# Linear attention feeding a gated MLP on one core: 128-row products for plain q and rest tokens, x normalised by pair, dependent transfers moved back in their queue

## The chip, the cores and the metric

The kernel runs on one core of one Trainium2 chip. A core has five engines, each with its own queue of instructions worked off in order: TensorE (PE, matrix products; PEld is its loading of weights), VectorE (DVE), ScalarE (ACT), GpSimd (POOL) and SyncE (SP), which here issues all DMAs. The metric is the device time of one execution in microseconds (us), as the median of several runs. The profile is of one further execution.

## The reference

Linear attention over 8 batches x 8 heads of 576 tokens with 64 features each, and then a gated MLP without an activation:

```python
def phi(x):
    proj = np.einsum('bhsd,df->bhsf', x, w_phi)                 # 64 -> 128 features
    proj = proj - np.max(np.abs(proj), axis=-1, keepdims=True)
    return np.concatenate([np.exp(proj), np.exp(-proj)], axis=-1)
q_p, k_p = (phi(q), phi(k))
kv = np.einsum('bhsf,bhsd->bhfd', k_p, v)
num = np.einsum('bhsf,bhfd->bhsd', q_p, kv)
den = np.einsum('bhsf,bhf->bhs', q_p, np.sum(k_p, axis=2))[..., None] + 1e-06
x = (num / den)                       # heads side by side: 4608 tokens x 512
out = (x @ w_a) * (x @ w_b) @ w_out   # 512 -> 1536 -> 512
```

All of it is in float32. The last three arrive as 64-bit numbers, which the kernel decodes to float32 itself.

## The kernel before

**Precision.** A product is either plain (float32 operands, each product two records on TensorE) or split: an operand is cut into a high and a low part (`split`, L146, with ScalarE's cast at L142 and VectorE's subtraction at L149; `stack`, L151, cuts one whose two copies lie in the two halves of the rows), and three products stand for one. The first 9 of 32 pairs of heads have plain k, q and numerators (`PLAIN_K`, `PLAIN_Q`, `PLAIN_NUM`, L38), the first 11 a plain kv.

**Attention.** It goes by pairs of heads (`attention_steps`, L386). For a pair, `k_chunks` (L258) makes features of k for 512 tokens in two chunks of 256 and adds their products with v to one PSUM tile `kvps` (`kv_add`, L292). The remaining 64 tokens of two pairs, the rest tokens, are put together as 128 rows (`rest_load`, `rest_chunk`): rows 0 to 63 are the first pair's, 64 to 127 the second's. `rest_add` (L280) takes one half of the rows, so these products have 64 rows. `k_finish` (L305) copies `kvps` (kvT), transposes it (`pt`, L314) and copies it again (kvh, L317). `q_side` (L325) goes by head: it loads q (L333; one transfer of 64 rows where q is plain, two copies in two transfers where it is split), multiplies with `w_phi` (`pq`, L346, 64 rows where plain), takes the greatest absolute value on GpSimd (`mb`, L350), subtracts it (L351), makes both exponentials (L354), multiplies with kv (`pn`, L370) and writes the numerators to `xun` and the denominators to `den`, both in DRAM. `reciprocals` (L376) loads a pair's denominators, inverts them and writes `rec` to DRAM.

**First pass of the MLP.** `load_weights` decodes the first 6 of 12 slices of w_a, w_b and w_out (18 tensors). `moe_block` (L566) works on 288 tokens, 16 blocks in all: `load_x` (L553) loads four chunks of x (`x_chunk`, L534: x unnormalised from `xun`, and `rec` broadcast over 64 rows in two transfers, then one multiplication on VectorE, L550) and splits them; for each slice `pa` and `pb` take 24 products (L583), are multiplied (L588) and split into hh and hl; then four output tiles `po` (L609) are summed, copied to `o` by ScalarE (L617), and the four are written to `part` in DRAM with one transfer (L624).

**Second pass.** The other 6 slices, on 512 tokens at a time, with Winograd's seven products (`second_pass`, L705; `winograd`, L660; x again through `x_chunk`, in `factors_of_x`, L626). Its weights are decoded and combined by `load_factors` while the last five blocks of the first pass run, partly set down in DRAM (`keep`) and fetched back (`fetch`). Its first tile `top` (L680) takes memory that the first pass's buffers held.

**What sets the order.** Attention is planned by hand in turns: a pair every 5 turns at first, then every 4; the constants at L24 to L35 give the turn of each step. Steps of the MLP are put into a deque and taken out at `PACE0` and then `PACE` steps a turn. Decoding is put there at turn 2, the two blocks of a batch `BLOCK_LAG` turns after its last pair's last step. This is the order in which the program names its instructions. The framework then sorts every engine's queue by a simulated timeline, an instruction named earlier going first among those that are ready, and the hardware works the queues off in that order.

Of the kernel before, what the change touches and what calls it, by code (L numbers as in the profile page):

```python
# [19 lines left out]
P = 128  # L20
EPS = 1e-6
# [12 lines left out]
DECODE_TURN, X_LAG, BLOCK_LAG = 2, 2, 8  # L34
PACE0, PACE, PACE0_UNTIL = 0.65, 0.9, 18  # L35
# [24 lines left out]
def tile_kernel(ctx, tc, qT, km, kr, vm, vr, w_phi, w_a, w_b, w_out, out):  # L60
# [14 lines left out]
    B, H, _, S = qT.shape  # L75
# [19 lines left out]
    rec = [dpool.tile([H, S], F32, name=f"rec{b}") for b in range(B)]  # L95
    part = dpool.tile([DM, NT], F32, name="part")
# [14 lines left out]
    def attention_consts(a1):  # L111
# [17 lines left out]
        make_identity(nc, ident)  # L129
        vaug = []  # L130
# [4 lines left out]
        return w2, wh, wl, wk32, wk2, ident, vaug  # L135
# [20 lines left out]
    def k_load(b, pr, a1, a2, ps, consts, st):  # L156
# [4 lines left out]
        if i < PLAIN_K:  # L161
            k32 = a1.tile([P, n], F32, tag="ks", bufs=2, name=f"k32_{u}")
            nc.sync.dma_start(k32, km[b, pr])
# [25 lines left out]
    def rest_load(b, g, a1, a2, ps, consts, st):  # L189
# [21 lines left out]
        if i >= PLAIN_KV:  # L211
            vh = a1.tile([P, 2, D + 1], F32R, tag="rvh", name=f"rvh_{u}")
            vl = a1.tile([P, 2, D + 1], F32R, tag="rvl", name=f"rvl_{u}")
            split(vh, vl, v32, engine("v_hi", b), engine("v_lo", b))
            st["rv", b, g] = (vh, vl)
# [109 lines left out]
    def q_side(b, pr, j, a1, a2, ps, consts, st):  # L325
        w2, wh, wl = consts[:3]
# [4 lines left out]
        q32 = a2.tile([P, S], F32, tag="q32", name=f"q32_{u}")  # L331
        for i in range(1 if plain_q else 2):
            nc.sync.dma_start(q32[i * D : (i + 1) * D], qT[b, h])  # L333
        yield
        if plain_q:
            parts = [(w2[:D], q32[:D])]
# [14 lines left out]
        engine("q_sub", b).tensor_tensor(p32, p32, mb, op=ALU.subtract)  # L351
# [20 lines left out]
        nc.sync.dma_start(xun[b][h * D : (h + 1) * D], xn[:D])  # L372
        nc.sync.dma_start(den[b][h : h + 1], xn[D : D + 1])
        yield

    def reciprocals(b, pr, a1):  # L376
        n = 2 * S // P
        hs = slice(2 * pr, 2 * pr + 2)
        r = a1.tile([P, n], F32, tag="rec", bufs=2, name=f"r_{b}_{pr}")
        nc.sync.dma_start(r, den[b][hs].rearrange("h (a n) -> (h a) n", n=n))  # L380
        nc.vector.tensor_scalar_add(r, r, EPS)
        nc.vector.reciprocal(r, r)
        nc.sync.dma_start(rec[b][hs].rearrange("h (a n) -> (h a) n", n=n), r)
        yield

    def attention_steps(pools, consts, st):  # L386
# [7 lines left out]
        for i in range(B * NPAIR):  # L394
# [13 lines left out]
            plan(reciprocals(b, pr, pools[0]), [t0 + Q_STEP + Q_TURNS[-1]])  # L408
            if b == 0:
                plan(x_first, [t0 + Q_STEP + Q_TURNS[-1] + X_LAG])  # L410
            if pr == NPAIR - 1:
                plan(b, [t0 + Q_STEP + Q_TURNS[-1]])
# [93 lines left out]
    def stage_shared(pool):  # L506

        def stage(kind, shape, dt, name):
            if kind == "raw":
                return xpool.tile(shape, dt, tag="o", bufs=2, name=name)  # L510
# [4 lines left out]
    def stage_second(xin, pool):  # L515

        tags = {"raw": (pool, "raw"), "w": (xin, "xs"), "w32": (xin, "rb"), "ws": (xin, "xs")}
# [16 lines left out]
    def x_chunk(p, j, c, pool, bufs):  # L534
# [3 lines left out]
        rb = pool.tile([P, T], F32, tag="rb", bufs=2, name=f"rb_{u}_{c}")  # L538

        t = j * T  # L540
        while t < (j + 1) * T:
            b, s0 = divmod(t, S)
            n = min(S - s0, (j + 1) * T - t)
            src, dst = slice(s0, s0 + n), slice(t - j * T, t - j * T + n)
            nc.sync.dma_start(x32[:, dst], xun[b][c * P : (c + 1) * P, src])
            for i in range(2):
                h = 2 * c + i
                nc.sync.dma_start(rb[i * D : (i + 1) * D, dst], rec[b][h : h + 1, src].broadcast_to([D, n]))
# [322 lines left out]
```

## Time and profile before

| | us |
|---|---|
| median of 3 runs | 1280.15 |
| lowest, highest | 1278.54, 1281.26 |
| profiled execution: span from first to last instruction | 1276.4 |
| TensorE busy | 1237.6 |
| TensorE loading weights | 1136.8 |
| VectorE busy | 928.9 |
| ScalarE busy | 733.0 |
| GpSimd busy | 155.4 |

The profiled execution is given by its span alone; the time of a run has a few microseconds more around it. Busy time of TensorE counts a record from its start to its modelled end, and records overlap: how close products follow each other is read from the times at which they start. A row such as `pq<-q,w 64*128 64x288` is a product into `pq` with weights of 64 rows and 128 columns, over 288 columns of data. A wait is written `<-` with the engine, the tile and the line that ended it.

### The profile page before, as it was taken

What the parts mean: (1) busy time and instruction counts of PE and PEld (TensorE: products, weight loads), DVE (VectorE), ACT (ScalarE), POOL (GpSimd) and SP (SyncE); (2) the same over time, 40 slices, a digit from 0 to 9 for tenths busy, and PEclk for the clock granted to TensorE, in tenths of its full rate; (3) what the DMA queues carried; (4) which work ended last, traced back from release to release, by engine and by line L of the source; (5) the groups of instructions that cost most, each with busy time, mean ns of one, the idle gap of its engine ahead of it and who ended that gap; (6) DMA issues with size and microseconds to landing.
All of it is one profiled execution on the core that took longest, in us unless ns stands there. A gap on an engine that the chain in (4) does not pass through costs nothing.

```text
span 1276.4 us, 23144 instructions
## 1 busy us (share of the span) xinstructions
PE 1237.6 (97%) x8588; PEld 1136.8 (89%) x8588; DVE 928.9 (73%) x1682; ACT 733.0 (57%) x1577; POOL 155.4 (12%) x70
## 2 busy tenths in 40 slices
PE   7899999999999999999999999889999999999998
PEld 4566789899999999999999999789999999999997
DVE  6989567998889999988965886824656556456443
ACT  5667668888888888988874444413223223223221
POOL 2332121212222221312220000000000000000000
PEclk9999999999999999999999999999999999999999
DMA  8665443353434434444225576791422322331221
GB/s 186 173 182 154 120 129 92 99 151 82 140 98 131 120 93 134 108 116 121 70 57 165 151 241 230 236 299 48 127 84 72 116 91 66 109 100 50 66 67 50
DMA packets 136656, 157.13 MB, mean 123 GB/s; under 512 B 40864, under 2 KB 93600, under 8 KB 136544
## 3 DMA queue, kind: packets, MB, share of 16 engines
q1 hardware_dynamic: 136544, 155.66, 42.4%
q8 instruction: 67, 1.10, 0.3%
q14 instruction: 45, 0.37, 0.1%
HBM read 117.56 MB, written 38.04 MB: 122 GB/s over the span
## 4 chain that ended last, share of the span: by engine, by line
PE 62%; DVE 14%; DMA 13%; ACT 6%; issue 4%; SPq 1%; DVEq 0%; ACTq 0%
PE pab L674 21%; PE po L721 11%; PE pa L583 6%; PE pb L583 5%; PE kvps L292 5%; PE po L609 5%; PE pn L370 4%; DMA x<-xun 3%; DMA rb<-rec 2%; PE pq L346 2%; DVE kd L240 1%; DMA raw_b<-in_w_b 1%; DVE qs L154 1%; DMA r<-den 1%; DVE kel L149 1%
## 5 line engine op out<-in xcount | busy, mean ns | idle before, releaser
L350 POOL PARTITION_ALL_REDUCE mb<-p x64 | 154.7, 2418 | 497.4 <-ACT p L347 463.2
L583 PE MATMUL pb<-xh,wh_b 128*128 128x288 f32 x384 | 115.6, 301 | 5.9 <-ACT o L617 2.9
L583 PE MATMUL pa<-xh,wh_a 128*128 128x288 f32 x384 | 116.0, 302 | 0.7 <-ACT xh L142 0.4
L583 PE MATMUL pb<-xh,wl_b 128*128 128x288 f32 x384 | 115.0, 299 | 0.0
L583 PE MATMUL pa<-xh,wl_a 128*128 128x288 f32 x384 | 115.0, 299 | 0.0
L609 PE MATMUL po<-hh,wh_o 128*128 128x288 f32 x384 | 110.3, 299 | 4.3 <-ACT hh L142 2.4
L583 PE MATMUL pa<-xl,wh_a 128*128 128x288 f32 x384 | 113.7, 296 | 0.0
L583 PE MATMUL pb<-xl,wh_b 128*128 128x288 f32 x384 | 113.3, 295 | 0.0
L609 PE MATMUL po<-hl,wh_o 128*128 128x288 f32 x384 | 112.2, 296 | 1.1 <-DVE hl L149 1.0
L609 PE MATMUL po<-hh,wl_o 128*128 128x288 f32 x384 | 112.4, 297 | 0.0
L142 ACT CAST hh<-h 128x288 fp32r<-128x288 f32 (+1 forms) x150 | 72.6, 503 | 68.7 <-DVE h L588 40.5
L149 DVE TENSOR_TENSOR hl<-h,hh 128x288 fp32r<-128x288 f32 (+1 forms) x150 | 81.7, 557 | 19.8 <-ACT hh L142 19.5
L550 DVE TENSOR_TENSOR x<-x,rb 128x288 f32<-128x288 f32 (+1 forms) x100 | 56.3, 567 | 53.4 <-DMA x<-xun 38.3
L583 PEld LDWEIGHTS pb<-xh,wh_b 128*128 128x128 f32 x384 | 72.6, 189 | 8.4 <-ACT h L587 4.6
L583 PEld LDWEIGHTS pa<-xh,wh_a 128*128 128x128 f32 x384 | 72.5, 189 | 4.6 <-issue 1.9
L609 PEld LDWEIGHTS po<-hh,wh_o 128*128 128x128 f32 x384 | 70.7, 188 | 5.9 <-ACT hh L142 3.1
L609 PEld LDWEIGHTS po<-hl,wh_o 128*128 128x128 f32 x384 | 72.4, 189 | 2.5 <-DVE hl L149 1.7
L583 PEld LDWEIGHTS pa<-xl,wh_a 128*128 128x128 f32 x384 | 73.4, 191 | 0.6 <-issue 0.2
L583 PEld LDWEIGHTS pa<-xh,wl_a 128*128 128x128 f32 x384 | 72.7, 189 | 1.3 <-issue 1.1
L583 PEld LDWEIGHTS pb<-xl,wh_b 128*128 128x128 f32 x384 | 73.4, 191 | 0.3
L583 PEld LDWEIGHTS pb<-xh,wl_b 128*128 128x128 f32 x384 | 72.8, 189 | 0.6 <-issue 0.6
L609 PEld LDWEIGHTS po<-hh,wl_o 128*128 128x128 f32 x384 | 71.9, 188 | 0.8 <-issue 0.8
(272 smaller groups left out, 3833.3 us busy)
## 6 DMA issues: line engine op xcount, KB each, us to landing
q<-in_qT SPq DMA_DIRECT2D x110, 144.0 KB
k<-in_km SPq DMA_DIRECT2D x55, 256.0 KB
xun<-xn SPq DMA_DIRECT2D x64, 144.0 KB
x<-xun SPq DMA_DIRECT2D x64, 144.0 KB
rb<-rec SPq DMA_DIRECT2D x128, 72.0 KB
part<-o SPq DMA_DIRECT2D x16, 576.0 KB
o<-part SPq DMA_DIRECT2D x36, 256.0 KB
out_x<-o SPq DMA_DIRECT2D x36, 256.0 KB
```

Source lines behind the costliest of these rows:

```text
L142: eng.copy(dst, src)
L149: eng_lo.tensor_tensor(lo, src, hi, op=ALU.subtract)
L154: eng_lo.tensor_tensor(hi_lo[D:], src[D:], hi_lo[D:], op=ALU.subtract)
L292: nc.tensor.matmul(st["kv_ps", b, pr][:width, j], v_[:, j, :width], e_[:, j], start=(left == NFULL and j == 0 and n_ == 0), stop=(left == ...
L346: nc.tensor.matmul(pq[:, :HALF], w_, q_[:, tok], start=(n_ == 0), stop=(n_ == len(parts) - 1))
L350: nc.gpsimd.partition_all_reduce(mb, p32, P, bass_isa.ReduceOp.absmax)
L370: nc.tensor.matmul(pn[: D + 1, :HALF], kv_[:, 2 * j + s, :], e_[:, s, tok], **at)
L550: nc.vector.tensor_tensor(x32, x32, rb, op=ALU.mult)
L583: nc.tensor.matmul(acc, w[:, cc * P : (cc + 1) * P], x, start=(k == 0), stop=(k == 3 * NCC - 1))
L609: nc.tensor.matmul(accs[cc], w[:, cc * P : (cc + 1) * P], h, **at)
L674: nc.tensor.matmul(acc[to][:, i], w_, x_, skip_group_check=True, **at)
L721: nc.tensor.matmul(acc[cc], w[:, cc * P : (cc + 1) * P], h, **at)
```

## The change

- Plain q: the two heads of a pair are loaded as one tile of 128 rows (`qP`), and multiplied with `wz[:, j]`, a copy of w_phi that is zero in the other head's rows (the tile that plain k already uses). Split q: the two copies come from the host as one tensor (`qD`) and one transfer.
- Rest tokens: v comes from the host with zeros in the other pair's 64 rows (`vr` has one more axis of 2), into two tiles that stay (`rvz`), and `rest_add` takes all 128 rows.
- x: `reciprocals` becomes seven steps. It loads the denominators, inverts them, writes `rec`, loads the pair's numerators (128 rows of 576), loads `rec` broadcast to the same shape, multiplies, and writes `xnorm` to DRAM. `x_chunk` loads from `xnorm` alone, in both passes. For this `xun` holds the two heads' rows in turn, and the host turns the rows of w_a and w_b the same way.
- Each of these transfers is named with `behind(loads, ...)`, and the two VectorE steps with `behind(marks, ...)`: `tc.issue_after` puts them behind the latest load of q or k, or the latest subtraction of q, in the queue of the same engine. It is an order in the queue and no wait on a semaphore. Steps lie up to 8 turns behind the pair's last step (2 in the first and the last batch).
- First pass: a block loads the next block's x while its own third slice runs (three chunks, the fourth when the first is split) and splits it among its outputs; `o` holds two output tiles and is written twice a block. The first block takes the decoding of w_out among its own steps; raw weights go through other buffers (qe and qel). Blocks are put in the deque 9 turns after a batch's last step (3 in the first and the last batch; before 8), at a `PACE` of 1.0 instead of 0.9.

```diff
-DECODE_TURN, X_LAG, BLOCK_LAG = 2, 2, 8
-PACE0, PACE, PACE0_UNTIL = 0.65, 0.9, 18
+REC_TURNS0, REC_TURNS, X_TURNS = (0, 1, 1, 1, 2, 2), (1, 3, 4, 5, 7, 8), (0, 1)
+DECODE_TURN, BLOCK_LAG = 2, 1
+PACE0, PACE, PACE0_UNTIL = 0.65, 1.0, 18
...
+        rvz = []
+        for i in range(2):
+            t = a1.tile([P, 2, 2, D + 1], F32, name=f"rvz{i}")
+            nc.vector.memset(t, 0.0)
+            for r in range(2):
+                nc.vector.memset(t[r * REST : (r + 1) * REST, r, :, D : D + 1], 1.0)
+            rvz.append(t)
...
-        v32 = a1.tile([P, 2, D + 1], F32, tag="rv32", name=f"rv32_{u}")
-        nc.vector.memset(v32[:, :, D : D + 1], 1.0)
-        nc.sync.dma_start(v32[:, :, :D], vr[b, g])
+        v32 = consts[6][g % 2]
+        nc.sync.dma_start(v32[:, :, :, :D], vr[b, g])
...
-        rows = slice(pr % 2 * REST, (pr % 2 + 1) * REST)
-        kv_add(b, pr, [v_[rows] for v_ in st["rv", b, pr // 2]], [e_[rows] for e_ in st["re", b, pr // 2]], st)
+        kv_add(b, pr, [v_[:, pr % 2] for v_ in st["rv", b, pr // 2]], st["re", b, pr // 2], st)
...
-            parts = [(w2[:D], q32[:D])]
+            parts = [(wz[:, j], st["q", b, pr])]
...
-        engine("q_sub", b).tensor_tensor(p32, p32, mb, op=ALU.subtract)
+        marks.append(nc.vector.tensor_tensor(p32, p32, mb, op=ALU.subtract))
...
+    def behind(what, issue):
+        with tc.issue_after(what[-1].ins):
+            issue()
...
         r = a1.tile([P, n], F32, tag="rec", bufs=2, name=f"r_{b}_{pr}")
-        nc.sync.dma_start(r, den[b][hs].rearrange("h (a n) -> (h a) n", n=n))
-        nc.vector.tensor_scalar_add(r, r, EPS)
+        behind(loads, lambda: nc.sync.dma_start(r, den[b][hs].rearrange("h (a n) -> (h a) n", n=n)))
+        yield
+        behind(marks, lambda: nc.vector.tensor_scalar_add(r, r, EPS))
         nc.vector.reciprocal(r, r)
-        nc.sync.dma_start(rec[b][hs].rearrange("h (a n) -> (h a) n", n=n), r)
+        yield
+        behind(loads, lambda: nc.sync.dma_start(rec[b][hs].rearrange("h (a n) -> (h a) n", n=n), r))
+        x32 = a1.tile([P, S], F32, tag="x32", name=f"x32_{b}_{pr}")
+        nc.sync.dma_start(x32, xun[b][rows])
+        yield
+        rb = a1.tile([P, S], F32, tag="rb", name=f"rb_{b}_{pr}")
+        behind(loads, lambda: nc.sync.dma_start(rb, rec[b][hs].unsqueeze(0).broadcast_to([D, 2, S])))
+        yield
+        behind(marks, lambda: nc.vector.tensor_tensor(x32, x32, rb, op=ALU.mult))
+        yield
+        behind(loads, lambda: nc.sync.dma_start(xnorm[b][rows], x32))
         yield
...
-            nc.sync.dma_start(x32[:, dst], xun[b][c * P : (c + 1) * P, src])
-            for i in range(2):
-                h = 2 * c + i
-                nc.sync.dma_start(rb[i * D : (i + 1) * D, dst], rec[b][h : h + 1, src].broadcast_to([D, n]))
+            nc.sync.dma_start(x32[:, t - j * T : t - j * T + n], xnorm[b][c * P : (c + 1) * P, s0 : s0 + n])
             t += n
-        nc.vector.tensor_tensor(x32, x32, rb, op=ALU.mult)
...
+            if f == 2 and j + 1 < blocks[0]:
+                loaded = [x_chunk(p, j + 1, c, pool, 3) for c in range(3)]
...
         for cc in range(NCC):
+            if loaded:
+                x_make(p, j + 1, cc, loaded.pop(0), pool)
+                if cc + 3 < NCC:
+                    loaded.append(x_chunk(p, j + 1, cc + 3, pool, 3))
             outputs(cc, range(NFS[p] - 1 if cc < ahead else 0, NFS[p]))
...
+            if cc % 2 == 0:
+                o = pool.tile([P, 2, T], F32, tag="o", bufs=2, name=f"o_{p}_{j}_{cc}")
+            nc.scalar.copy(o[:, cc % 2], acc)
+            if cc % 2:
+                nc.sync.dma_start(dst[:, cc - 1 : cc + 1], o)
...
+    def first_block(block, decodes):
+        for steps in decodes:
+            yield from steps
+            next(block)
+            yield
+        yield from block
```

More of the change, by code (lines that the diff above doesn't have):

```diff
@@ L59, in tile_kernel @@
 @with_exitstack
-def tile_kernel(ctx, tc, qT, km, kr, vm, vr, w_phi, w_a, w_b, w_out, out):
+def tile_kernel(ctx, tc, qP, qD, km, kr, vm, vr, w_phi, w_a, w_b, w_out, out):
     nc = tc.nc
-    B, H, _, S = qT.shape
+    B, H, _, S = qD.shape
     NPAIR = H // 2
@@ L211, in rest_load @@
         if i >= PLAIN_KV:
-            vh = a1.tile([P, 2, D + 1], F32R, tag="rvh", name=f"rvh_{u}")
-            vl = a1.tile([P, 2, D + 1], F32R, tag="rvl", name=f"rvl_{u}")
+            vh = a1.tile([P, 2, 2, D + 1], F32R, tag="rvh", name=f"rvh_{u}")
+            vl = a1.tile([P, 2, 2, D + 1], F32R, tag="rvl", name=f"rvl_{u}")
             split(vh, vl, v32, engine("v_hi", b), engine("v_lo", b))
@@ L567, in moe_block @@
         T, pool = TS[p], xpools[p]
-        xs = first_x if (p, j) == (0, 0) else list(load_x(p, j, pool))
-        hs = []
+        if j not in block_x:
+            for c in range(NCC):
+                x_make(p, j, c, x_chunk(p, j, c, pool, 3), pool)
+        xs, hs, loaded = block_x.pop(j), [], []
         psum = pools_moe[-1]
@@ L592, in moe_block @@
             hs.append((hh, hl))
+            if f == 2 and j + 1 < blocks[0]:
+                loaded = [x_chunk(p, j + 1, c, pool, 3) for c in range(3)]
             yield
-        cols = slice(j * T, (j + 1) * T)
-        o = pool.tile([P, NCC, T], F32, tag="o", bufs=2, name=f"o_{p}_{j}")
-        dst = (part if p == 0 else out).rearrange("(c p) s -> p c s", p=P)[:, :, cols]
-        last = p > 0 and cols.stop == NT
-        if p > 0:
-            nc.sync.dma_start(o, part.rearrange("(c p) s -> p c s", p=P)[:, :, cols])
+        dst = part.rearrange("(c p) s -> p c s", p=P)[:, :, j * T : (j + 1) * T]
         accs = {}
@@ L767, in tile_kernel @@
     away = {}
-    weights, pools_moe, xpools, first_x = {}, [ps_moe], [xpool], []
+    weights, pools_moe, xpools, block_x, blocks, marks, loads = {}, [ps_moe], [xpool], {}, [0], [], []
     per = S // TS[0]
@@ L773, in tile_kernel @@
         work, tasks, due, st = deque(), {}, 0.0, {}
-        tasks[DECODE_TURN] = []
-        for names in ("ab", "o"):
-            stage = stage_shared(pools[1])
-            tasks[DECODE_TURN] += [whole(load_weights(0, f, nm, stage, home(f, nm))) for f in range(NFS[0]) for nm in names]
+        stage = stage_shared(pools[1])
+        decodes = {nm: [whole(load_weights(0, f, nm, stage, home(f, nm))) for f in range(NFS[0])] for nm in "abo"}
+        tasks[DECODE_TURN] = [decodes[nm][f] for f in range(NFS[0]) for nm in "ab"]
         for turn, ready in attention_steps(pools, consts, st):
@@ L781, in tile_kernel @@
                 tasks[at] = [moe_block(0, ready * per + h) for h in range(per)]
+                if ready == 0:
+                    tasks[at][0] = first_block(tasks[at][0], decodes["o"])
+                blocks[0] += per
             for t in sorted(tasks):
```

76 lines of the change are left out of this document (41 added, 35 removed).

## The prediction, made before the result

> **What bounds the kernel now.** I read the page first, then the stages in the view of windows, then TensorE's timeline, the waits and SyncE's timeline around the places that stand out.
>
> ```profile
> span 1276.4 us, 23144 instructions
> PE 62%; DVE 14%; DMA 13%; ACT 6%; issue 4%; SPq 1%; DVEq 0%; ACTq 0%
> ```
>
> The chain that ended last lies on TensorE for 62%, and on VectorE and DMAs for 27%. The windows say where. Columns: microseconds, then busy time and records of PE, PEld, DVE, ACT, POOL, then the granted clock, the DMA share and GB/s.
>
> ```profile
> 0.00:192.00 192.00, 178.15 (x885) 123.48 (x886) 148.22 (x285) 127.67 (x280) 50.41 (x27) 0.98 0.60 157
> 192.00:768.00 576.00, 568.53 (x4297) 551.38 (x4296) 503.55 (x877) 457.15 (x997) 104.96 (x43) 1.00 0.43 120
> 768.00:864.00 96.00, 83.43 (x601) 81.51 (x601) 55.36 (x124) 33.33 (x80) 0.00 (x0) 0.96 0.78 258
> 864.00:1277.00 413.00, 407.52 (x2811) 380.46 (x2809) 221.81 (x398) 114.85 (x222) 0.00 (x0) 1.00 0.26 80
> ```
>
> Four stages: a start, where attention and the decoding of the first weights share the engines (TensorE idle for 13.9 us); the middle, attention beside blocks of the first pass and then blocks alone (7.5 us idle in 576); a transition, where the second pass's weights are made (12.6 in 96, DMA share 0.78); the second pass (5.5 in 413, most of it at the kernel's end). From 192 to 768 us and again from 864 us TensorE sets the time. There a wait of another engine is worth little, but a product that takes longer than it must costs its full price, and busy time doesn't show that. The records' start times do.
>
> **The change, part by part.**
>
> *Products of 128 rows.* Columns of the timeline: start, duration of the row, operation, rows*columns of the weights, count.
>
> ```profile
> 22.85 1.89 PE L292 MATMUL kvps<-ke,v 128*65 128x256 f32 x8
> 24.58 2.10 PE L370 MATMUL pn<-qe,kvh 128*65 128x288 f32 x8
> 26.52 1.03 PE L225 MATMUL pk<-wk,k 128*128 128x256 f32 x4
> ```
>
> ```profile
> 12.96 1.03 PE L225 MATMUL pk<-wk,k 128*128 128x256 f32 x4
> 13.92 1.23 PE L346 MATMUL pq<-q,w 64*128 64x288 f32 x4
> 15.09 1.13 PE L225 MATMUL pk<-wk,k 128*128 128x256 f32 x4
> 16.15 1.08 PE L292 MATMUL kvps<-ke_r,rv 64*65 64x256 f32 x4
> 17.15 1.73 PE L292 MATMUL kvps<-ke,v 128*65 128x256 f32 x7
> ```
>
> ```profile
> 509.93 0.29 PE L346 MATMUL pq<-qs,wl 128*128 128x288 f32 x1
> 510.16 0.33 PE L292 MATMUL kvps<-keh_r,rvh 64*65 64x256 f32 x1
> 510.42 0.40 PE L583 MATMUL pb<-xl,wh_b 128*128 128x288 f32 x1
> 510.65 0.29 PE L583 MATMUL pb<-xh,wl_b 128*128 128x288 f32 x1
> 510.78 0.30 PE L583 MATMUL pb<-xh,wh_b 128*128 128x288 f32 x1
> ```
>
> ```profile
> 660.20 0.28 PE L292 MATMUL kvps<-keh_r,rvl 64*64 64x256 f32 x1
> 660.32 0.27 PE L292 MATMUL kvps<-keh_r,rvh 64*65 64x256 f32 x1
> ```
>
> The first three rows follow each other without a break: eight products of 256 columns in 1.73 us, 0.216 each, and eight of 288 columns in 1.94, 0.242 each. The split ones start 0.12 us (660.20 to 660.32) and 0.13 us apart (510.65 to 510.78). So four pk from 12.96 should let the next start at 13.83; it starts at 13.92, 0.09 late. The four pq should end their turn at 14.89; the next starts at 15.09, 0.20 late. Four pk on, 15.95 becomes 16.15, again 0.20; and the four rest products let the next start 0.14 late. Each lateness stands at a change between 64 and 128 rows, on either side of it. One run of 64-row products in plain form thus costs 0.09 on entry, 0.20 on leaving it, and the 0.1 that the first product after it loses: 0.40 us for q, by the same reading 0.29 for rest tokens. In split form the rest product due at 510.06 started at 510.16, the pb due at 510.28 at 510.42, and the next one lost another 0.10, together 0.34 us.
>
> ```profile
> L346 PE MATMUL pq<-q,w 64*128 64x288 f32 x72 | 24.9, 446 | 2.7 <-DMA q<-in_qT 1.5 <-ACT xn L371 1.0 <-PE pk L225 0.2
> L292 PE MATMUL kvps<-ke_r,rv 64*65 64x256 f32 x48 | 13.1, 389 | 0.0
> L292 PE MATMUL kvps<-keh_r,rvh 64*65 64x256 f32 x40 | 12.0, 301 | 0.0
> ```
>
> The 72 records of plain q come in 23 runs, the 48 of plain rest tokens in 11, the 120 split ones (three groups of 40) in 25: 59 runs, as counted along the timeline, from the first q to the one with the two rows at 660. 23 x 0.40 + 11 x 0.29 + 25 x 0.34 = 20.9 us. 27 of the runs begin after 192 us, nearly all split: 27 x 0.34 = 9 us, on the path; I take 8, since a few runs stand where TensorE waits anyway. The other 32 runs, about 12 us, lie in the start, where VectorE is busy 77% of the time and some of the room will be filled by waiting: I take 6 (bounds 0 and 12). The new products have as many columns, so they take no more. The Trainium skill, "TensorEngine Tiling (Array Packing)", section "Theoretical Speedup", speaks against padding: with a contraction of 64 rows, two row tiles can work at once, for up to twice the speed. In this trace the 64-row products start as far apart as 128-row ones of the same width, so none is side by side with another. By that rule padding would throw away half of their time; that is a rival below.
>
> *x normalised by pair.*
>
> ```profile
> L550 DVE TENSOR_TENSOR x<-x,rb 128x288 f32<-128x288 f32 x64 | 31.5, 498 | 32.2 <-DMA x<-xun 25.5 <-DMA rb<-rec 6.0 <-issue 0.5
> L550 DVE TENSOR_TENSOR x<-x,rb 128x512 f32<-128x512 f32 x36 | 24.8, 688 | 21.2 <-DMA x<-xun 12.7 <-DMA rb<-rec 7.8 <-issue 0.5
> L351 DVE TENSOR_TENSOR p<-p,mb 128x576 f32<-128x576 f32 x64 | 51.2, 801 | 2.0 <-POOL mb L350 1.5 <-issue 0.5
> ```
>
> 100 multiplications (56.3 us busy, and 53.4 us in which VectorE stood before them) become 32 over 128x576, by the third row 0.80 us each: 25.6. In the second pass TensorE hides all of it: 0. In the middle it is worth the share of TensorE's 7.5 idle microseconds that VectorE's standing causes: 2 (0 to 6). 256 broadcast loads of rec go, 32 x 3 transfers come (x unnormalised, rec, x normalised). The chain from a pair's last product to x gets two steps longer, a write to DRAM and a load. The nearest rows, from the chain in time:
>
> ```profile
> 209.88 3.62 DMA x<-xun
> 271.26 2.05 DMA rb<-rec
> ```
>
> Two such steps are 4 to 7 us, and the new steps are planned up to 8 turns behind the products. For all batches but the first the blocks are queued about as late as before (9 turns against 8) behind a backlog of blocks: 0. The first batch has no backlog; its blocks are queued 5 turns earlier, and w_out's decoding stands among the first block's steps instead of before them, which takes six decodings out of VectorE's way there. These two pull against each other; I take 0 (7 us worse to 5 better).
>
> *Loads of q, and the padded v of the rest tokens.* 55 transfers fewer (110 to 55), on a queue that is off TensorE's path; the rest's v doubles to 128 KB in 16 transfers, and the two splits of each of 10 groups to 260 columns. All of it lies under TensorE's work: 0. Without that cover the splits would cost, by the two rows of the multiplication (0.19 us for 224 columns more), 20 x 0.11 = 2 us.
>
> *Transfers behind named instructions.* No wait is added: a dependent transfer stands later in its queue, behind a load of q or k that is already issued, and the multiplication behind a subtraction of q. What was queued behind the waiting transfer (loads of q, k, v, writes of xun) gets through sooner. Behind the moved multiplication on VectorE stand the splits of h; they wait for data that was asked for turns before. 0 by itself.
>
> *The transition.* Blocks now load x one block ahead, from one tensor, and write their partial sums in two halves. Waits between 768 and 862 us, then the queues around 845 us:
>
> ```profile
> DVE x L550 <- DMA x<-xun: 12.0, 5, 7.3
> DVE x L550 <- DMA rb<-rec: 5.9, 3, 2.9
> PE pab L674 <- ACT top L680: 4.4, 1, 4.4
> PE pb L583 <- ACT o L617: 2.9, 1, 2.9
> ```
>
> ```profile
> 843.57 1.41 SPq L548 DMA_DIRECT2D rb<-rec  x2
> 845.07 1.83 SPq L531 DMA_DIRECT2D back_b_s<-kept_wf_q_b_s  x2
> 848.90 0.38 SPq L624 DMA_DIRECT2D part<-o  x1
> ```
>
> ```profile
> 845.16 0.40 ACT L617 COPY o<-po 128x288 f32<-128x288 f32 x1 [1.99 <-PE po L609]
> 856.10 1.07 ACT L680 COPY top<-pab 128x512 f32<-128x512 f32 x2 [10.54 <-DMA back_h<-kept_wh_o]
> ```
>
> The last block's copy was done at 845.56; its 576 KB write was issued only at 848.90, behind loads of rec and of weights, and ScalarE could write top, which takes the old buffers' place, at 856.10. TensorE lost 4.4 us. With no rec loads and half of the bytes already gone, I expect some 2 to 4 of that back. TensorE lost the 2.9 us to copies of o behind ScalarE's casts of x, which waited for VectorE's multiplication, which waited for x. That chain loses its middle. Of the stage's 12.6 idle microseconds, and the clock's 0.04 x 96 = 3.8, I take 8 (2 to 14).
>
> The clock has a price of its own. It falls behind stalls of TensorE:
>
> ```profile
> 54.63 1.99 PE L370 MATMUL pn<-qe,kvh 128*65 128x288 f32 x4 [2.53 <-ACT kvh L317]
> ```
>
> The four products behind this one take 1.99 us, where eight took 2.10 at 24.58. By the granted clock the start loses 0.02 x 192 = 3.8 us. The Trainium skill, "TensorE: Matmul & The Clock Gate", section "Why this matters for your kernels", says that it takes gaps above about 3 us. Here 2.53 us was enough, so the measurement decides. By the page only the 4.4 us stall would count, and 8 for the transition would be about 6. I leave the start's loss in, since nothing in the change touches ScalarE's kvh.
>
> Sum: 8 + 6 + 2 + 8 = 24 us off the span: 1252.4. The median of the runs, 1280.15, lies 3.75 above the span, so the time is **1256 us**.
>
> **The rivals.**
>
> *Little gain.* The late starts don't belong to the 64 rows, or the start and the transition fill the freed time with VectorE's and the DMAs' own work. Against it: 128-row products of three kinds follow each other on time (22.85 to 26.52), whatever their widths. For it: 32 of 59 runs lie in the start. Then 8 us remain: 1272.
>
> *More.* The start gains its whole 12 us and half of what the clock takes (2), the transition 14, the middle 6, with the 8: 42. 1238.
>
> *Slower.* ScalarE's casts of x now stand among the copies of a block's output. If x is late there, all copies behind the cast wait, the PSUM buffers stay full, and TensorE stands as it did for the 2.9 us above, once a block. 15 of 16 blocks are loaded this way; all of them late would cost 15 x 2.9 = 43 us: 1299. It decides from 24 / 2.9, about 8 blocks, on. For it: three buffers, and the fourth chunk is asked for only when the first is split. Against it: that leaves three outputs of 18 products, 3 x 18 x 0.133 = 7 us, and an x load took 3.6.
>
> *The row rule.* If 64-row products could go side by side, padding them would lose half of their time: (72 x 0.242 + 48 x 0.216 + 120 x 0.12) / 2 = 21 us, and 1277. Nothing in the trace shows two at once.
>
> **How the numbers follow.** Forecast 0.55, little gain 0.20, more 0.15, slower 0.07, row rule 0.03. Range 1238 to 1272: it takes in more and little gain, and leaves out the slower case and the tails. 0.2% is 2.6 us, about what a measurement of this kernel can tell. Faster: 0.55 + 0.19 + 0.15 = 0.89. Same: the row rule and a rest of little gain, 0.04. Slower 0.07.
>
> **What would show it.** Right: no 64-row shape among TensorE's groups, and products around the rest tokens starting 0.12 us apart; TensorE's records in a window of the middle up by some 2%; 32 multiplications of 128x576 and no rec load by halves; no stall of 4 us where top is first written. Wrong: idle time of TensorE before a block's pa or pb with ScalarE's copy of o or cast of x as its end; a first block that begins later by more than the start gains; lateness that stays with 128-row products. If the start alone doesn't shrink, VectorE bound it; if the middle doesn't, the 64 rows weren't the cause.

## The result, and the profile after

| | before | after |
|---|---|---|
| median of 4 runs, us | 1279.93 | 1257.98 |
| lowest, highest | 1278.54, 1281.26 | 1255.87, 1260.3 |
| span of the profiled execution | 1276.4 | 1257.4 |

The ratio is 0.9821, with an interval of 0.9802 to 0.9841: faster by 1.8%, two microseconds from the forecast of 1256. The sum came out right; several of its terms did not, and they made up for each other. Below, a difference between two variants is the difference of their ratios to the kernel before, each measured on its own chip, times 1280 us. A profile is of one execution of a variant, which can lie some microseconds from the median.

The head of the page and its chain, for the kernel after:

```profile
span 1257.4 us, 22777 instructions
PE 66%; DMA 12%; DVE 11%; ACT 7%; issue 3%; SPq 1%; POOL 0%; ACTq 0%; DVEq 0%
```

The same four windows, with the same columns as before (the last ends with this span):

```profile
0.00:192.00 192.00, 169.45 (x860) 126.64 (x861) 147.89 (x276) 123.40 (x273) 47.85 (x27) 0.96 0.64 183
192.00:768.00 576.00, 567.81 (x4365) 561.06 (x4364) 513.58 (x866) 465.84 (x1018) 106.34 (x44) 1.00 0.51 149
768.00:864.00 96.00, 93.41 (x695) 91.83 (x694) 52.04 (x111) 34.66 (x80) 0.00 (x0) 0.98 0.64 219
864.00:1258.00 394.00, 388.62 (x2673) 362.41 (x2671) 195.28 (x351) 108.46 (x208) 0.00 (x0) 1.00 0.21 65
```

Read the counts, not the busy time. In the middle TensorE gets through 4365 records instead of 4297, with 0.7 us less busy time. In the transition it gets through 695 instead of 601. By 192 us, though, it is 25 records behind: the start became worse.

TensorE's timeline at a rest token's products in split form, in the kernel after:

```profile
508.46 0.28 PE L299 MATMUL kvps<-keh,vl 128*64 128x256 f32 x1
508.58 0.28 PE L299 MATMUL kvps<-keh_r,rvh 128*65 128x256 f32 x1
...
509.17 0.28 PE L299 MATMUL kvps<-keh_r,rvl 128*64 128x256 f32 x1
509.29 0.29 PE L357 MATMUL pq<-qs,wh 128*128 128x288 f32 x1
509.41 0.29 PE L357 MATMUL pq<-qs,wl 128*128 128x288 f32 x1
```

They follow one another 0.11 to 0.12 us apart, into the run and out of it: the lateness is gone, as is every 64-row shape among plain q and the rest tokens. The groups of the multiplication and of ScalarE's cast of x (busy time and mean ns of one, then the idle time before it and what ended it):

```profile
L409 DVE TENSOR_TENSOR x<-x,rb 128x576 f32<-128x576 f32 x32 | 24.2, 755 | 14.5 <-DMA xun<-xn 7.3 <-DMA rb<-rec 6.6 <-issue 0.6
L151 ACT CAST xh<-x 128x288 fp32r<-128x288 f32 x64 | 25.9, 443 | 20.1 <-DMA x<-xnorm 20.0
```

The second row is the wait that the rival "slower" named: ScalarE stands 20 us before casts of x that has not come. TensorE's waits show next to nothing behind it. The transition, in TensorE's waits between 760 and 870 us:

```profile
PE po L633 <- ACT hh L151: 1.0, 1, 1.0
PE pab L699 <- ACT top L705: 1.0, 1, 1.0
PE po L633 <- DVE hl L158: 0.6, 1, 0.6
```

The stall before the second pass's first tile has shrunk from 4.4 us to 1.0, and the 2.9 us behind copies of o are gone. This table, from the starts of TensorE's products, says where the variants of the next section part (microseconds; "block" is one of the first pass's 16):

| | before | after | e1 | e2 | e3 | e4 | e12 |
|---|---|---|---|---|---|---|---|
| first head's numerators | 26.3 | 30.6 | 29.8 | 31.0 | 24.8 | 29.6 | 24.3 |
| end of block 1 | 165.4 | 168.8 | 172.0 | 167.6 | 165.9 | 167.0 | 143.8 |
| end of block 2 | 225.0 | 225.0 | 229.3 | 227.0 | 222.0 | 225.1 | 202.4 |
| end of block 11 | 687.7 | 682.8 | 688.4 | 697.2 | 681.0 | 711.2 | 669.4 |
| second pass begins | 845.0 | 831.0 | 834.6 | 852.2 | 826.5 | 861.2 | 824.6 |
| last product | 1271.1 | 1252.2 | 1256.1 | 1280.5 | 1246.6 | 1282.2 | 1258.5 |

Before against after: nothing won by the end of block 2; 4.9 us from there to block 11 (462.7 against 457.8); 9.1 from there to the second pass (157.3 against 148.2); 4.9 within it. Together 18.9. Profiles of kernels that hardly differ here show how far one stretch can be trusted: from block 2 to 11 e3, e7, e9 and e10 take 456.7 to 459.0 us, from there to the second pass 145.5 to 147.9.

Why the start is worse shows in two engines' timelines. TensorE's, with its wait in brackets, and then ScalarE's, both of the kernel after:

```profile
17.24 1.13 PE L357 MATMUL pq<-q,wk 128*128 128x288 f32 x4
24.25 0.67 PE L321 MATMUL pt<-ident,kvT 65*128 65x65 f32 x4 [5.87 <-ACT kvT L317]
24.70 3.62 PE L299 MATMUL kvps<-ke,v 128*65 128x256 f32 x8
```

```profile
9.94 0.89 ACT L358 COPY p<-pq 128x288 f32<-128x288 f32 x2 [0.27 <-PE pq L357]
...
22.38 0.68 ACT L365 ACTIVATE qe<-p 128x576 f32<-128x576 f32 x1 [5.69 <-DVE p L362]
22.97 0.67 ACT L366 ACTIVATE qe<-p 128x576 f32<-128x576 f32 x1
23.54 0.56 ACT L317 COPY kvT<-kvps 65x512 f32<-65x512 f32 x1
```

The copy that TensorE needs stands on ScalarE behind two exponentials, which wait for VectorE's subtraction, which waits for GpSimd. Behind this stall eight products take 3.62 us instead of 1.89: the clock has fallen (granted 0.50 from 23 to 29 us). GpSimd's first all-reduce, in its timeline:

```profile
18.21 4.30 POOL L361 PARTITION_ALL_REDUCE mb<-p  x2 [9.75 <-issue]
```

Its data is there at 10.83 (9.94 + 0.89 above); it begins at 18.21, after a wait for nothing that the profile shows. In the kernel before, it is as late (17.99 us). What differs there is the order on ScalarE, by its timeline of before:

```profile
21.86 0.58 ACT L310 COPY kvT<-kvps 65x512 f32<-65x512 f32 x1
22.34 0.68 ACT L354 ACTIVATE qe<-p 128x576 f32<-128x576 f32 x1
```

The copy stands ahead of the exponentials, and TensorE waits 0.79 us for it instead of 5.87. A second stall of 4.58 us stands at 103 us, behind ScalarE's decoding of w_out, which waits 3.59 us for its raw weights among the first block's steps.

### The profile page after: what moved, and what is told of

It is laid out like the page before. It is cut to its first block, busy times and chain, and to the rows that moved or that the text cites. A ratio compares the mean times of both kernels' runs of the same rounds, so it can differ in the third digit from the quotient of the medians.

```text
span 1257.4 us, 22777 instructions
## 1 busy us (share of the span) xinstructions
PE 1219.3 (97%) x8588; PEld 1141.9 (91%) x8588; DVE 908.8 (72%) x1604; ACT 732.4 (58%) x1577; POOL 154.2 (12%) x70
## 4 chain that ended last, share of the span: by engine, by line
PE 66%; DMA 12%; DVE 11%; ACT 7%; issue 3%; SPq 1%; POOL 0%; ACTq 0%; DVEq 0%
PE pab L699 21%; PE po L746 11%; PE pa L610 7%; PE pb L610 7%; PE po L633 6%; PE kvps L299 6%; PE pn L381 5%; PE pq L357 2%; DMA rec<-r 1%; DMA x<-xnorm 1%; DMA r<-den 1%; DMA kept_wf_q_a_s<-wf_q_a_s 1%; DVE kd L248 1%; PE pk L242 1%; DMA rb<-rec 1%
## 5 line engine op out<-in xcount | busy, mean ns | idle before, releaser
L158 DVE TENSOR_TENSOR qel<-qe,qeh 128x1152 fp32r<-128x1152 f32 x46 | 63.3, 1376 | 12.6 <-ACT qeh L151 12.2
```

The costliest lines, as they stand in the source:

```text
L158: eng_lo.tensor_tensor(lo, src, hi, op=ALU.subtract)
```

## The experiments

**e1: the change without padding.** Plain q and rest tokens multiply 64 rows again; all else as after.

```diff
-            parts = [(wz[:, j], st["q", b, pr])]
+            half = slice(j * D, (j + 1) * D)
+            parts = [(consts[0][half], st["q", b, pr][half])]
...
-        kv_add(b, pr, [v_[:, pr % 2] for v_ in st["rv", b, pr // 2]], st["re", b, pr // 2], st)
+        rows = slice(pr % 2 * REST, (pr % 2 + 1) * REST)
+        kv_add(b, pr, [v_[rows, pr % 2] for v_ in st["rv", b, pr // 2]], [e_[rows] for e_ in st["re", b, pr // 2]], st)
```

> The changed kernel, with its loads as they are, but with plain q and rest tokens multiplied over 64 rows again (the same data, so the same result). Theory: each of some 59 runs of 64-row products costs 0.29 to 0.40 us of TensorE's time; the 27 in the middle are on the path, about 9 us; the 32 in the start are not, because VectorE, ScalarE and GpSimd bound it. So 9 us slower than the changed kernel, about 1267, and 192 us hold the same records as without. Rival: the start's are on the path too and were hidden by two new stalls: 18 to 20 us slower, about 1277, with some 60 records fewer by 192 us. Second rival, after the row rule of the Trainium skill, TensorEngine Tiling (Array Packing), Theoretical Speedup: as q's two heads now lie in different halves of the rows, their products overlap; then pq products start less than 0.242 us apart and the kernel is no slower than 1260.

Measured (here and below the median, the lowest and highest run, and the ratio with its interval): 1262.12 (1260.8 to 1263.39), ratio 0.9878 (0.9863 to 0.9892): slower than after by 7 us by ratios, 4 by medians, and still 16 us faster than before. The lateness came back, as TensorE's timeline of e1 shows:

```profile
513.13 0.28 PE L300 MATMUL kvps<-keh,vl 128*64 128x256 f32 x1
513.33 0.33 PE L300 MATMUL kvps<-keh_r,rvh 64*65 64x256 f32 x1
513.50 0.28 PE L300 MATMUL kvps<-kel_r,rvh 64*65 64x256 f32 x1
...
513.97 0.28 PE L300 MATMUL kvps<-keh_r,rvl 64*64 64x256 f32 x1
514.18 0.40 PE L359 MATMUL pq<-qs,wh 128*128 128x288 f32 x1
514.42 0.30 PE L359 MATMUL pq<-qs,wl 128*128 128x288 f32 x1
```

0.20 and 0.17 us on entry instead of 0.12, 0.21 and 0.24 on leaving. Over the 26 runs after 192 us this adds up to some 8.7 us, the 9 of the prediction. But from block 2 to block 11 e1 takes only 1.3 us longer than after (459.1 against 457.8), no more than kernels with the same products differ there. This stretch of after, and then of e1, in the columns of the windows:

```profile
225.00:682.80 457.80, 450.30 (x3492) 445.79 (x3491) 410.92 (x645) 393.76 (x846) 99.71 (x41) 1.00 0.50 141
229.30:688.40 459.10, 455.85 (x3492) 445.18 (x3491) 410.88 (x645) 393.91 (x844) 98.93 (x41) 0.95 0.50 141
```

For the same number of records TensorE is busy 5.5 us less with padding, and stands 4.2 us more (7.5 against 3.3). So the lateness belongs to the 64 rows, and in the middle most of the time won turned into waiting. In the start e1 shows something else, on TensorE's timeline:

```profile
79.59 0.56 PE L359 MATMUL pq<-q,w 64*128 64x288 f32 x1
79.60 0.70 PE L300 MATMUL kvps<-ke_r,rvz 64*65 64x256 f32 x2
79.99 0.41 PE L359 MATMUL pq<-q,w 64*128 64x288 f32 x1
80.13 0.39 PE L300 MATMUL kvps<-ke_r,rvz 64*65 64x256 f32 x1
80.24 0.41 PE L359 MATMUL pq<-q,w 64*128 64x288 f32 x1
80.36 0.39 PE L300 MATMUL kvps<-ke_r,rvz 64*65 64x256 f32 x1
80.49 0.42 PE L359 MATMUL pq<-q,w 64*128 64x288 f32 x1
80.84 0.88 PE L300 MATMUL kvps<-ke,v 128*65 128x256 f32 x3
```

Four products of q and four of rest tokens, on different halves of the rows, go side by side; the first two begin within 0.01 us of each other. All eight are through in 1.25 us (79.59 to 80.84), where one after the other, as far apart as plain products are in this profile, they would take 4 x 0.251 + 4 x 0.224 = 1.90. The two heads of a q, which the expectation named, are never found side by side. In the table e1 is 4.3 us behind after by the end of block 2 already, and 3.9 at the end. But how the 4 to 7 us divide between the start and the rest can't be read from this profile: its granted clock was 0.949, at which plain products, nearly all of them in the start, begin 4% further apart.

**e2: padding alone, in the kernel before.**

```diff
...
-        for i in range(1 if plain_q else 2):
-            nc.sync.dma_start(q32[i * D : (i + 1) * D], qT[b, h])
+        if plain_q:
+            if j == 0:
+                st["q", b, pr] = a2.tile([P, S], F32, tag="q32", name=f"q32_{u}")
+                nc.sync.dma_start(st["q", b, pr], qT[b, 2 * pr : 2 * pr + 2].rearrange("h d s -> (h d) s"))
...
-            parts = [(w2[:D], q32[:D])]
+            parts = [(wz[:, j], st["q", b, pr])]
...
-        kv_add(b, pr, [v_[rows] for v_ in st["rv", b, pr // 2]], [e_[rows] for e_ in st["re", b, pr // 2]], st)
+        kv_add(b, pr, [v_[:, pr % 2] for v_ in st["rv", b, pr // 2]], st["re", b, pr // 2], st)
```

> The kernel before, with 128-row products alone (q in pairs, zeros in v of the rest tokens), and x, the order of the transfers and the blocks as before. Theory: the middle gains 8 to 9 us and the start nothing: about 1271. Rival: the rows give all of the 20.9 us that the runs cost: 1259, which would be the whole of the change. If it is below 1265, the other parts of the change are worth less than the transition's share says.

Measured: 1281.6 (1276.96 to 1287.9), ratio 1.0033 (1.0015 to 1.0051). No gain at all, a loss of 4 us instead. The twelve runs spread over 11 us, and the profile is of the longest, 1287.9, 6 us above the median. The row of the start's stall, in e2's timeline of TensorE, is the one that after shows too:

```profile
24.38 0.67 PE L319 MATMUL pt<-ident,kvT 65*128 65x65 f32 x4 [5.60 <-ACT kvT L315]
```

The kernel before has no such stall there; its first numerators are done at 26.3, those of e2 at 31.0. e1, whose loads are those of after but whose products have 64 rows, has the stall too (4.39 us). So what brings it isn't the 128-row products themselves; it comes with their loads or with the order that the framework makes, and no run tells these two apart. From block 2 to 11 e2's profile takes 470.2 against 462.7, of which those 6 us may be a part. Products that follow each other faster gave nothing by themselves in the kernel before.

**e5 and e6: load added to one engine.** e5 is after with one more subtraction of 128x288 on VectorE for each head with a split q; e6 has each product of a split q twice.

```diff
+        if not plain_q:
+            nc.vector.tensor_tensor(mb[:, :HALF], p32[:, :HALF], mb[:, :HALF], op=ALU.subtract)
```

```diff
+                if not plain_q:
+                    for w_, q_ in parts:
+                        nc.tensor.matmul(pq[:, :HALF], w_, q_[:, tok], start=True, stop=True)
```

> The changed kernel with one more subtraction of 128x288 on VectorE for each of the 46 split heads (into a tile that nobody reads again): 46 x about 0.48 = 22 us of VectorE's time, all in the middle and around it. New theory, after the runs with 64 rows and with free order: the middle is held by VectorE's queue, which is busy or standing nearly all the time, and TensorE has room: most of it shows, 14 to 22 us slower than the changed kernel, 1272 to 1280. Rival, the recorded one: TensorE sets the time there: 0 to 5 us, at most 1263.

> The changed kernel with each product of split q made twice, the first time to no effect: 46 heads x 2 halves x 2 products x 0.13 = 24 us of TensorE's time in the same stretch. VectorE theory: TensorE's room takes much of it, up to 10 us slower, 1268 at most. Rival (TensorE sets the time): 20 to 24 us, 1278 to 1282. If both this and the other addition show in full, the two engines hold each other in turn.

The added subtractions, as a group of e5, and two groups of e6 (the first of each pair of products; they are 184 records, and products of this width start about 0.13 us apart, so 24 us):

```profile
L364 DVE TENSOR_TENSOR mb<-p,mb 128x288 f32<-128x288 f32 x46 | 24.5, 532 | 0.2
```

```profile
L358 PE MATMUL pq<-qs,wh 128*128 128x288 f32 x92 | 27.8, 302 | 1.0 <-DVE qs L163 1.0
L358 PE MATMUL pq<-qs,wl 128*128 128x288 f32 x92 | 27.1, 295 | 0.0
```

Measured: e5 1267.41 (1264.18 to 1271.43), ratio 0.9922 (0.9903 to 0.9941), 13 us over after; e6 1269.6 (1267.9 to 1273.06), ratio 0.9942 (0.9925 to 0.9959), 15 over after. Of 24 us added to either engine, about half to two thirds shows, and each of the two differences is uncertain by some 3.5 us. If TensorE alone set the time, e5 would show nothing; if VectorE alone did, e6 would show nothing. So neither does: each holds the other in turn. The profiles show it in different places. In e6 the stretch from block 2 to 11 gets 12.3 us longer (470.1). In e5 it hardly does (459.5), but attention, which runs beside the blocks, has its last product at 695.8 instead of 676.2, and the loss shows behind block 11. That the 9 us of lateness were worth even less than added products (1.3 of 8.7) fits a TensorE that waits for VectorE in between, but these two runs don't show why it was so little.

**e4, e7 and e8: the named order.** e4 issues all that `behind` handles without an order; e7 keeps the order for the two VectorE steps alone; e8, with `marks` in place of `loads` in the second diff, for the transfers alone.

```diff
     def behind(what, issue):
-        with tc.issue_after(what[-1].ins):
-            issue()
+        issue()
```

```diff
     def behind(what, issue):
+        if what is loads:
+            issue()
+            return
```

> The changed kernel without the named instructions: the same steps on the same turns, but nothing is put behind a load or a subtraction. Theory: TensorE sets the time in the middle, so VectorE's and SyncE's standing costs little there: 0 to 3 us slower, 1258 to 1261. Rival: the order is what gave the transition its gain and the middle part of its: 8 us slower or more, 1266 and above, with VectorE standing before the multiplication for some 30 us.

> The changed kernel with the named instructions on VectorE alone: the two steps stay behind a subtraction of q, the DMAs are free. VectorE theory: what cost 29 us without any order was VectorE standing in front of the multiplication for rec and xun; with its own queue in order it stands less, and most comes back: 1258 to 1268. Rival: the transfers' order in SyncE's queue is what matters (a free dependent transfer stands there ahead of loads): 1275 or more.

> The changed kernel with the named instructions on the DMAs alone: transfers stay behind loads, VectorE's two steps are free. VectorE theory: the simulated timeline then puts the multiplication where it believes the data to be there, VectorE stands before it: 1275 or more. Rival (SyncE's order matters): 1258 to 1268.

Measured: e4 1287.24 (1284.36 to 1289.98), ratio 1.0074 (1.0057 to 1.009): 32 us slower than after, and slower than before. e7 1256.68 (1253.96 to 1259.79), ratio 0.9841 (0.982 to 0.9863): as after. e8 1267.29 (1263.44 to 1271.56), ratio 0.9922 (0.9902 to 0.9941): 13 us slower than after. VectorE's order gives all of it; that of the transfers gives 19 of the 32 where VectorE's is missing, and nothing that can be measured where it is there. The middle's window and VectorE's waits in it, in e4:

```profile
192.00:768.00 576.00, 547.30 (x4121) 535.04 (x4120) 483.74 (x807) 449.19 (x977) 100.63 (x44) 0.99 0.47 136
```

```profile
DVE x L408 <- DMA rb<-rec: 32.3, 16, 5.2
DVE r L398 <- DMA r<-den: 14.5, 13, 3.3
```

In the kernel after, these two are 6.6 and 8.6 us over the whole kernel (and 7.3 more for `xun`, whose load is the one transfer of the chain that `behind` doesn't handle), and here 46.8 in the middle alone. The expectation of 0 to 3 us failed; its rival had VectorE's standing right, though not the transition. The multiplication of e4 stands in VectorE's queue ahead of work that is ready, before its transfer has come, and VectorE stands with it. TensorE gets through 244 records fewer. From block 2 to 11 it takes 486.1 us against 457.8; the later stages are as in after (150.0 and 421.0). In e8 VectorE stands 16.4 us in the middle for `r`, twice as long as in after (8.3).

**e11: the named order alone, in the kernel before.**

```diff
-        engine("q_sub", b).tensor_tensor(p32, p32, mb, op=ALU.subtract)
+        marks.append(nc.vector.tensor_tensor(p32, p32, mb, op=ALU.subtract))
...
-        nc.vector.tensor_scalar_add(r, r, EPS)
+        with tc.issue_after(marks[-1].ins):
+            nc.vector.tensor_scalar_add(r, r, EPS)
...
-        nc.vector.tensor_tensor(x32, x32, rb, op=ALU.mult)
+        with tc.issue_after(marks[-1].ins):
+            nc.vector.tensor_tensor(x32, x32, rb, op=ALU.mult)
...
```

> The kernel before, with nothing changed but the order on VectorE: its multiplications of x and its additions to the denominators are named behind the latest subtraction of q. Theory from the runs with parts of the order: VectorE's queue is what the middle gains by, and before the change it stood 15 us for DMAs between 192 and 640 us; half of that shows, 5 to 9 us faster than before: 1269 to 1274. Rival: the order is only needed for the new, longer chain and the old one was well placed: 1276 to 1281, or slower, since the multiplications of the second pass and of the transition get no useful mark.

Measured: 1335.55 (1334.34 to 1337.27), ratio 1.0455 (1.043 to 1.048): 4.5% slower than before, where 5 to 9 us faster was expected. TensorE's middle has 3878 records instead of 4297. VectorE's wait for `xun` there does fall, from 20.1 us to 9.1. But TensorE stands 22.2 us before attention's products for ScalarE's copies kvT and kvh, instead of 2.1. One reading is that the multiplication is a block's own step there, asked for when the block needs it, and that the step and all that hangs on it come late when it is held behind the latest subtraction; the rows don't show this chain. What is shown is that the order didn't pay without the plan of turns.

**e9 and e10: the transition.** e9 writes a block's four output tiles at once again; e10 loads x at the block's start again.

```diff
-            if cc % 2 == 0:
-                o = pool.tile([P, 2, T], F32, tag="o", bufs=2, name=f"o_{p}_{j}_{cc}")
+            if cc == 0:
+                o = pool.tile([P, NCC, T], F32, tag="o", bufs=1, name=f"o_{p}_{j}")
...
```

```diff
-            if f == 2 and j + 1 < blocks[0]:
+            if False:
```

> The changed kernel with a block's four output tiles in one buffer, written once, as before the change (here with one such buffer instead of two). Theory: the 4.4 us in which TensorE stood where top is first written came from the size and place of the last block's write; it returns for the most part, with the clock's dip, and blocks wait a little for the one buffer: 3 to 6 us slower than the changed kernel, 1261 to 1264, with a stall of 3 us or more before top. Rival: the stall went because the loads of rec between went: no stall, 1256 to 1259.

> The changed kernel with every block loading and splitting its own x when it begins, none ahead. Theory: the transition's gain of some 9 us lies in x being there when it is split; without it the transition (from the end of block 11 to the first pab) goes from 148 back to 153 to 157 us, and the time to 1263 to 1267. Rival: the gain lies in the multiplications and the rec loads that went: 1257 to 1260.

Measured: e9 1258.54 (1255.46 to 1261.48), ratio 0.9852 (0.9827 to 0.9878); e10 1255.72 (1253.53 to 1258.21), ratio 0.9829 (0.9806 to 0.9851). Neither can be told from after. From block 11 to the second pass e9 takes 147.9 us and e10 146.1, against 148.2 after and 157.3 before, and the stall before top is 0.83 us in e9. Neither the halved write nor the loading ahead made the transition shorter. Padding didn't either: e1 takes 146.2 without it, e2 155.0 with it. What is left of the change there is above all that the blocks' loads of rec and their multiplications are gone. That these are the cause is what remains by exclusion: no run took them alone, and the pace of the blocks and the buffers of the raw weights changed too.

**e3: GpSimd's first call at the start.** After, with a call on two columns ahead of everything:

```diff
...
+        warm = a1.tile([P, 4], F32, name="warm")
+        nc.gpsimd.memset(warm[:, :2], 0.0)
+        nc.gpsimd.partition_all_reduce(warm[:, 2:], warm[:, :2], P, bass_isa.ReduceOp.absmax)
```

> The changed kernel, with one small all-reduce on GpSimd as the first thing in its queue, so that whatever delays the first all-reduce until 18.2 us (its data was there at 10.8) is over before q comes. Theory: the start is bound by what follows GpSimd's first reduce: it begins at 11 to 12 us, TensorE's stall of 5.9 us at 18 us goes, and 5 to 8 us come off, about 1251. Rival: the start is bound by VectorE's decoding of weights; the reduce begins earlier, the stall goes, but the first block's end at 169 us moves by less than 2 us, and the time by less than 2.

Measured: 1251.29 (1246.03 to 1254.22), ratio 0.9779 (0.9756 to 0.9803): 5 us faster than after by ratios, 7 by medians, and the lowest median of all. The two intervals just touch (0.9802 and 0.9803), so the runs alone don't settle that it is faster than after. What the call does is clear, in GpSimd's timeline of e3:

```profile
1.09 0.37 POOL L132 PARTITION_ALL_REDUCE warm<-warm  x1
...
11.72 2.14 POOL L364 PARTITION_ALL_REDUCE mb<-p  x1 [10.02 <-ACT p L361]
```

The first call with data now begins 6.5 us sooner and waits for data alone. The stall before pt falls from 5.87 to 1.93 us, block 1 ends 2.9 us sooner, and the last product 5.6. But e10, which has no early call and can't be told from after, ends block 1 at 165.2 and has its last product at 1246.2, as early as e3. So the shorter stall is shown; that it makes the whole kernel faster isn't.

**e12: e3 with w_out's decoding where it was.**

```diff
-        tasks[DECODE_TURN] = [decodes[nm][f] for f in range(NFS[0]) for nm in "ab"]
+        tasks[DECODE_TURN] = [decodes[nm][f] for f in range(NFS[0]) for nm in "ab"] + decodes["o"]
...
-                if ready == 0:
-                    tasks[at][0] = first_block(tasks[at][0], decodes["o"])
```

> The changed kernel with the early small all-reduce on GpSimd, and with w_out's decoding back among the tasks of turn 2, ahead of the first block. Theory: TensorE's stall of 4.6 us at 103 us stood behind ScalarE, which waited 3.6 us for a raw w_out; with the decoding out of the first block it goes, and 3 to 5 us come off the 1251 of the early all-reduce: 1246 to 1249. Rival: VectorE's decoding then delays the first block's h by as much or more: 1251 to 1256.

Measured: 1268.33 (1265.62 to 1270.27), ratio 0.9929 (0.9908 to 0.995): 19 us slower than e3, which I had not expected. The stall at 103 us went, and block 1 ended 22 us sooner. But attention's last product moved from 674.4 to 697.7, and TensorE waits again at the second pass's first tiles:

```profile
PE pab L702 <- ACT top L708: 4.9, 1, 4.9
PE pab L702 <- ACT xth L154: 3.7, 1, 3.7
```

From the second pass's beginning to its end it takes 433.9 us against 420.1. It looks as if the earlier blocks took their time from attention, whose end then fell into the making of the second pass's weights; no run tests that.

## Why the prediction was right, and where it was not

**The forecast's total** was off by 2 us of a gain of 22. By stages it was 6 us for the start, 10 for the middle and 8 for the transition; the profiles have 0, 4.9 and 14.0 (9.1 up to the second pass, 4.9 in it). That these add up to nearly the same is luck.

**128-row products, 14 us.** Mis-sized. The lateness was read rightly: it is in e1 and gone in after. Priced nearly at full in the middle and at half in the start, it should have given 14 us; e1 puts it at 4 to 7, and in the middle, where the forecast had 8, at 1.3 in one profile. The step that failed is "There a wait of another engine is worth little, but a product that takes longer than it must costs its full price". TensorE's 99% of busy time in the middle hid that VectorE, busy for 87% of it, holds it in between (e5), so that time won on TensorE became waiting: 4.2 us of 5.5 in e1's stretch. In the old kernel padding gave nothing (e2).

**The row rule.** "Nothing in the trace shows two at once" was wrong. It holds for the products that the prediction quoted, which were of one kind and on one half. Where q met rest tokens of the other half, the trace of before has them side by side, as TensorE's timeline around 30 us shows:

```profile
30.03 0.43 PE L292 MATMUL kvps<-ke_r,rv 64*65 64x256 f32 x1
30.04 0.51 PE L346 MATMUL pq<-q,w 64*128 64x288 f32 x1
30.30 0.38 PE L292 MATMUL kvps<-ke_r,rv 64*65 64x256 f32 x1
30.39 0.40 PE L346 MATMUL pq<-q,w 64*128 64x288 f32 x1
30.51 0.59 PE L292 MATMUL kvps<-ke_r,rv 64*65 64x256 f32 x2
31.03 0.94 PE L370 MATMUL pn<-qe,kvh 128*65 128x288 f32 x3
```

Six products take 1.00 us instead of 4 x 0.216 + 2 x 0.242 = 1.35. This happens three times in before (at 30, 62 and 142 us) and four times in e1, so by these rows padding gave away about 1 us: halves do go side by side, but the two kinds seldom meet. The Trainium skill, "TensorEngine Tiling (Array Packing)", section "Theoretical Speedup", gives a dimension of 64 up to twice the speed, and these rows agree in kind. The Trainium skill says in the same page's section "Key Properties" that changing the tiling mode drains TensorE; the trace agrees there too in that products start late at each change of rows, about 0.3 us for a run of 64-row products. Whether halves could be made to meet on purpose, 72 products of plain q two at a time, was not tried.

**Transfers and VectorE's steps behind named instructions: "0 by itself".** Wrong, and the largest miss. Inside the new structure VectorE's order is worth 32 us (e4, e7). Without any order the chain of seven steps makes the kernel slower than before: that was the missing rival on the slow side. The forecast came out all the same, as the change has the order in it. The estimate looked at what is queued behind a moved step, and not at what the step would stop if it weren't moved.

**x normalised by pair: 2 us in the middle.** From block 2 to 11, e1, which has all but padding, takes 3.6 us less than before (459.1 against 462.7): in its bounds of 0 to 6, with the order's help, and with the blocks' new pace, which no run took alone. In the second pass, 0 was right for the multiplications; its 4.9 us are mostly the stall before top (4.4 to 1.0) and the clock that fell behind it.

**The first batch, 0 (7 worse to 5 better).** Block 1 ended 3.4 us later and block 2 at the same time: right within its bounds. The 6 us of gain for the start did not come. In its place stand a stall of 5.87 us that the trace of before doesn't have, behind a copy that now follows the exponentials on ScalarE, another of 4.58 among w_out's decodings, and a granted clock of 0.96 instead of 0.98.

**The transition, 8 (2 to 14).** 9.1 us to the second pass's beginning, and most of the 4.9 behind it: 13, at its upper end. Of the reasons given, the half writes and the loading ahead fall (e9, e10); the rec loads and multiplications are what is left, not shown by a run of their own.

**Slower.** Its wait was there, 20.0 us on ScalarE, in 14 waits, the longest 2.4 us. The three outputs of 18 products between ask and use, which spoke against it, seem to have covered them.

What stays open: why padding gave the old kernel nothing (e2). Every edit lets the framework sort all queues anew, and no run separates the two. The pace of the blocks (1.0 instead of 0.9) was not taken back alone either. Whether e12's earlier blocks could be had without the later attention was not tried.

## What to carry to other kernels

Before pricing a gain on one engine at full, add a known load to each of the two busiest engines. If less than all of it shows, a saving is worth less than its full price too, and it can be worth less still: here 15 of 24 us of added products showed, but 1.3 of 8.7 us of lateness taken away in the middle. On an engine that works its queue off in order, a step that waits for a chain of transfers should be planned turns after its data was asked for and named behind work that is ready; in this kernel the naming without the planning cost more than it saved (e11), and so did the planning without the naming (e4). Where an engine's first call of a kind starts late with nothing to wait for, a call at the start on a few columns can take the delay away (e3); whether the kernel gets faster by it is a second question.

## What the runs showed of the hardware

- GpSimd's first all-reduce begins 6 to 7 us after its data is there (17.99 against 11.69 in before, 18.21 against 10.83 in after), and an earlier call on two columns takes that away. The Trainium skill, "GPSIMD Engine Reference", section "2.1 Instruction dispatch", gives the first call of freshly loaded code some 6 us that no row shows; the traces agree in kind, and nearly in size.
- Products on the two halves of the rows go side by side (e1: eight in 1.25 us instead of 1.90), and a change between 64 and 128 rows delays the products around it, by some 0.33 us for a run of 64-row products in split form (e1).
- The granted clock was 0.949 in nearly all of e1's profiled execution. Split products began as far apart as at 1.00 (0.13 us for 288 columns); plain ones 0.224 us for 256 columns instead of 0.216, and 0.251 for 288 instead of 0.242. The execution, 1263.39 us, was as long as another of e1 at a clock of 0.992, 1263.25.
